# W2 by seven block products in place of eight, in a DeltaNet and MLP kernel

## The chip, the cores and the metric

The kernel runs on one core of one Trainium2 chip. The metric is the device time of one execution in microseconds (us). Before the change, six runs gave a median of 615.64 us, between 613.14 and 621.12.

## The reference

There are two stages. The first is a delta-rule recurrence, for 4 batches and 8 heads of width 48 over 768 tokens; the second is a layer norm and an MLP of width 384 to 1536 to 384 with a residual. All is float32.

```python
for t in range(S):
    kt, vt, bt = (k_n[:, :, t], v[:, :, t], beta[:, :, t, None])
    y[:, :, t] = np.einsum('bhd,bhde->bhe', q[:, :, t], state)
    v_old = np.einsum('bhde,bhd->bhe', state, kt)
    state = state + bt[:, :, :, None] * np.einsum('bhd,bhe->bhde', kt, vt - v_old)
...
x = np.ascontiguousarray(attn_out.transpose(0, 2, 1, 3)).reshape(B, S, H * D)
...
xn = (x - mu) / np.sqrt(var + 1e-06) * g_ln
ch = np.maximum(xn @ w_ch1, 0.0) @ w_ch2
return (x + ch).astype(np.float32)
```

## The kernel before

**Chunks.** The 768 tokens are cut into 12 chunks of 64 (C). A chunk has 256 rows for the MLP (TOK: 4 batches of 64 tokens), in two groups g of 128. Within a chunk the recurrence is made parallel: products of keys with keys and queries with keys (`gram` L368, `product` L393), the inverse of a triangular matrix per head, and a few small matmuls with the carried state s_all.

**The inverse.** From chunk 4 on, two chunks are inverted together in blocks of 32 by a loop on VectorE: 31 steps of one multiply (tmp, L555) and one subtract (xb, L560). Chunks 0 to 3 use blocks of 16, joined to 32 first. At the end `scatter` turns the result (own, L483), fills xt (L468, L472), and `join` (L574 to L631) makes the full block of 64 with two sets of small matmuls on TensorE (p_e L580, p_z L626); x_n (L574) is what p_e multiplies with.

**The recurrence.** `recur` has, for every chunk, p_k and p_y from the state (L652), VectorE's subtraction from v (L657), p_u (L663), the state's update p_s (L675) with VectorE's addition to s_all (L678), the second part of p_y (L683), and then the layer norm's numbers (L694 to L701) and the transposition of its result (p_n, L709; xnt, L710).

**The MLP.** `ffn(c)` first makes h, in 12 blocks of 128 columns: three matmuls into p_h (L724) and ScalarE's Relu into a tile h_f (L730). Then it makes h W2: for each group g, twelve matmuls 128 rows by 384 columns are added up in one PSUM accumulator p_o (L746). VectorE adds the residual x into o (L735), and SyncE stores it in two transfers (L737). Chunk 0 does both groups together, the other chunks one after the other. p_h and p_o take turns in two PSUM buffers (tag "ffn").

**Weights.** W1 and W2 come as 64-bit words and are turned into float32 by ScalarE and VectorE while the first chunks run (`to_fp32`, L313 to L326); the pool "early" holds the raw words and is closed when that is done.

**Order.** The kernel's first part has an order written out by hand. After it, a `Plan` gives every piece of work a due time on a line of its own, where one chunk of the recurrence takes T = 45 steps, and issues the pieces in order of due time. `ffn(c)` is spread in N_FFN = 24 turns (12 for h, 12 for the product) over the T steps that follow the start of chunk c + 1. The inverse of a pair due at t runs from t - 58 to t - 18, its join until t - 2. The framework derives the waits, and on each engine instructions run in the order in which they were queued. VectorE, GpSimd and SyncE are such queues; SyncE carries the loads of q, k and v together with the stores, GpSimd the loads of turned k, the scaling of v (L428) and some clearings.

Of the kernel before, what the change touches and what calls it, by code (L numbers as in the profile page):

```python
# [8 lines left out]
FP32 = mybir.dt.float32  # L9
U32 = mybir.dt.uint32  # L10
U16 = mybir.dt.uint16
ALU = mybir.AluOpType
ACTF = mybir.ActivationFunctionType
# [3 lines left out]
C = 64  # L17
# [76 lines left out]
def kernel(  # L94
# [22 lines left out]
    nc = tc.nc  # L117
# [3 lines left out]
    DM = H * D  # L121
    DFF = w_ch1.shape[1]
    KC = DM // 128
    FT = DFF // 128
    NP = H // 2
    GH = 2 * H
    TOK = 256
# [3 lines left out]
    work = ctx.enter_context(tc.tile_pool(name="work", bufs=2))  # L131
# [15 lines left out]
    def ps_ffn(shape, name):  # L147
        return psum.tile(shape, FP32, name=name, tag="ffn", bufs=2)
# [61 lines left out]
    w2_sb = const.tile([128, FT, DM], FP32, name="w2_sb")  # L210
# [73 lines left out]
    for t in kraws:  # L284
# [5 lines left out]
        out=is_b, in_=ident.rearrange("p (q b s) -> p b q s", b=2, s=FB), axis=mybir.AxisListType.XY, op=ALU.add  # L290
    )
    nc.vector.tensor_reduce(
        out=is_u, in_=ident.rearrange("p (e u s) -> p u e s", u=2, s=BK), axis=mybir.AxisListType.XY, op=ALU.add
# [144 lines left out]
    def prep_v(c):  # L438
        if c > 2:
            load_kv(c)  # L440
        yield
        scale_v(c, norms(c), nc.gpsimd)
        yield
# [267 lines left out]
        yield  # L711


    N_FFN = FT + 2 * FT // 2

    mlp = {}

    def ffn(c):
        xnt, x = xnts.pop(c), xs.pop(c)
        hs = []  # L720
        for f in range(FT):
            p_h = ps_ffn([128, TOK], "p_h")
            for t in range(KC):
                nc.tensor.matmul(  # L724
                    p_h, w1_sb[:, t, f * 128 : (f + 1) * 128], xnt[:, t],
                    start=(t == 0), stop=(t == KC - 1),
                )
            mlp["PE"] = nc.cur_bb.bb.instructions[-1]
            h_f = work.tile([128, TOK], FP32, name="h_f", bufs=FT)
            nc.scalar.activation(h_f, p_h, ACTF.Relu)  # L730
            hs.append(h_f)
            yield
        def store(g, p_o):
            o = work.tile([128, DM], FP32, name="o", bufs=2)
            nc.vector.tensor_tensor(out=o, in0=p_o, in1=x[:, g], op=ALU.add)  # L735
            for e in range(2):
                nc.sync.dma_start(  # L737
                    out=out[2 * e + g, c * C : (c + 1) * C, :], in_=o[e * C : (e + 1) * C]
                )


        for gs in ((0, 1),) if c == 0 else ((0,), (1,)):
            p_os = [ps_ffn([128, DM], "p_o") for g in gs]
            for f in range(FT):
                for g, p_o in zip(gs, p_os):
                    nc.tensor.matmul(  # L746
                        p_o, hs[f][:, g * 128 : (g + 1) * 128], w2_sb[:, f],
                        start=(f == 0), stop=(f == FT - 1),
                    )
                mlp["PE"] = nc.cur_bb.bb.instructions[-1]  # L750
                if f % 2 and f < FT - 1:
                    yield
            for g, p_o in zip(gs, p_os):
                store(g, p_o)
            yield


    NW = len(pieces)
# [88 lines left out]
        load_kv(2)  # L847
        load_beta()

    T = 45  # L850
    starts = [0, 14, 64] + [80 + T * i for i in range(NCH - 2)]
    ends = [2, 26, 80] + starts[4:]
    plan = Plan()
    plan.spread(weights(3, NW // 2), NW // 2 - 3, 0, 10)
    plan.spread(weights(NW // 2, NW), NW - NW // 2, 12, 38)

    plan.once(39, early.close)
    for c in range(NCH):
        t0, t1 = starts[c], ends[c]
        if c > 1:  # L860
            plan.spread(prep_v(c), 2, t0 - 72, t0 - 12)
        if c:
            plan.once(t0, begin, c)
        plan.spread(recur(c) if c else recur_0, N_RECUR if c else 1, t0, t1)
    plan.spread(second(), 7, 0, 14)
    ffn_0 = ffn(0)
    plan.spread(ffn_0, FT, 2, 18, whole=False)
    plan.spread(ffn_0, FT // 2, 20, 42)
    plan.spread(ffn(1), N_FFN, 42, 80)
    for c in range(2, NCH):  # L870
        plan.spread(ffn(c), N_FFN, starts[c + 1], starts[c + 1] + T)
    for m in range(1, NSL):
        chunks = range(SLAB * m, SLAB * m + SLAB)
        t = starts[SLAB * m]
# [55 lines left out]
```

## Time and profile before

| | |
|---|---|
| median of six runs | 615.64 us |
| the profiled execution, its own time | 618.93 us |
| its span, first to last instruction | 617.0 us |
| mean granted TensorE clock | 0.977 |
| TensorE busy, matmuls | 542.7 us |
| of it p_h (L724), 864 matmuls | 208.1 us |
| of it p_o (L746), 576 matmuls | 201.2 us |
| VectorE busy | 322.3 us |
| ScalarE busy | 170.3 us |
| GpSimd busy | 80.0 us |

The profile names the engines PE (TensorE; PEld is its loading of weights), DVE (VectorE), ACT (ScalarE), POOL (GpSimd) and SP (SyncE). The profiled execution is one run, 3.3 us above the median. A row of slices shows 40 equal parts of the span, 15.4 us each, with the busy share in tenths. A group of instructions shows line, engine, operation, output and inputs by the program's names, shapes and count, then busy time and mean length of one in ns, then the idle time of the engine before them and what ended it. A float32 matmul of the code is two matmuls in the profile, and a matmul's recorded length overlaps that of the next, so the step from start to start is what one costs.

### The profile page before, as it was taken

To read this page: it belongs to the slowest core of one execution; us is meant where nothing else is said; L and a number is where in the kernel's file an instruction comes from. 1 tells how busy PE (TensorE), PEld (TensorE's weight loads), DVE (VectorE), ACT (ScalarE), POOL (GpSimd) and SP (SyncE) were. 2 spreads that over 40 slices of the span, in tenths; PEclk is the share of its full clock that TensorE was granted. 3 is DMA by queue.
4 is the path that set the end of the run, shared out by engine and by line. 5 is a ranking of instruction groups with operands and counts; after the bars stand their busy time and mean duration, and the time that the engine had idled before them with its cause. 6 is when DMAs were issued, how large, how long until landed. Compare 5 with 4: busy or idle time off the path is not lost.

```text
span 617.0 us, 20905 instructions
## 1 busy us (share of the span) xinstructions
PE 542.7 (88%) x9512; PEld 405.9 (66%) x9512; DVE 322.3 (52%) x681; ACT 170.3 (28%) x351; POOL 80.0 (13%) x128
## 2 busy tenths in 40 slices
PE   2045886889999959999999999999999999999997
PEld 2035675557767746866857867768758678677673
DVE  5844868992236994229973149953179730201000
ACT  1222352403333205241314332242322142112120
POOL 5000116331040302300302300011000010000000
PEclk9999989988999988999999999999999999999999
DMA  4716979426034610411510510200200000000101
GB/s 53 183 57 150 186 165 242 71 52 97 5 65 78 105 14 18 85 34 27 91 28 16 89 29 15 53 15 16 53 14 15 1 16 15 14 15 1 27 1 26
DMA packets 126919, 34.51 MB, mean 56 GB/s; under 512 B 121184, under 2 KB 124272, under 8 KB 126832
## 3 DMA queue, kind: packets, MB, share of 16 engines
q1 hardware_dynamic: 110256, 19.14, 18.6%
q0 software_dynamic: 3504, 10.25, 6.2%
q10 hardware_dynamic: 13072, 3.80, 2.7%
q8 instruction: 74, 1.21, 0.8%
q14 instruction: 13, 0.11, 0.1%
HBM read 28.44 MB, written 4.72 MB: 54 GB/s over the span
## 4 chain that ended last, share of the span: by engine, by line
PE 57%; DVE 26%; issue 7%; DMA 3%; ACT 3%; SPq 2%; POOL 1%; ACTq 0%; DVEq 0%; POOLq 0%
PE p_h L724 21%; PE p_o L746 19%; DVE tmp L555 8%; DVE xb L560 8%; PE p_g L393 2%; PE p_e L580 2%; PE p_y L683 2%; PE p_g L368 2%; PE p_z L626 2%; DVE kqt L348 2%; PE p_u L663 1%; DVE own L483 1%; SPq L168 1%; PE p_n L709 1%; PE p_s L675 1%
## 5 line engine op out<-in xcount | busy, mean ns | idle before, releaser
L724 PE MATMUL p_h<-xnt,w_sb 128*128 128x256 f32 x864 | 208.1, 395 | 5.5 <-DVE o L735 4.8
L746 PE MATMUL p_o<-w_sb,h_f 128*128 128x384 f32 x576 | 201.2, 498 | 0.0
L724 PEld LDWEIGHTS p_h<-xnt,w_sb 128*128 128x128 f32 x864 | 165.5, 196 | 33.7 <-DVE o L735 4.0
L746 PEld LDWEIGHTS p_o<-w_sb,h_f 128*128 128x128 f32 x576 | 107.5, 193 | 65.5 <-issue 2.7
L730 ACT ACTIVATE h_f<-p_h 128x256 f32<-128x256 f32 x144 | 55.3, 384 | 193.4 <-PE p_h L724 193.4
L168 POOL DMA_DIRECT2D tb<-in_k_dram x64 | 41.9, 662 | 111.1 <-DVE tmp L555 57.3
L560 DVE TENSOR_TENSOR xb<-xb,tmp 128x31 f32<-128x31 f32 (+20 forms) x154 | 51.1, 332 | 5.1
L735 DVE TENSOR_TENSOR o<-p_o,x_ln 128x384 f32<-128x384 f32 x24 | 13.2, 549 | 74.1 <-PE p_o L746 74.1
L555 DVE TENSOR_TENSOR tmp<-xb,gb 128x31 f32<-128x31 f32 (+15 forms) x124 | 42.3, 341 | 3.8
L694 DVE BATCH_NORM_STATS2 st<-x_ln 128x6 f32<-128x384 f32 x24 | 12.3, 546 | 51.5 <-ACT x_ln L688 51.5
L678 DVE TENSOR_TENSOR s_all<-s_all,p_s 128x768 f32<-128x768 f32 x11 | 10.3, 940 | 47.4 <-PE p_s L675 47.2
L348 DVE STREAM_TRANSPOSE kqt<-tb 128x1024 f32<-128x1024 f32 x24 | 29.3, 1231 | 4.1 <-DMA tb<-in_k_dram 3.8
L368 PE MATMUL p_g<-kqt 48*64 48x64 f32 (+2 forms) x1024 | 16.5, 234 | 13.1 <-DVE kqt L348 8.2
L368 PEld LDWEIGHTS p_g<-kqt 48*32 48x32 f32 (+1 forms) x1024 | 14.4, 130 | 18.6 <-DVE kqt L348 8.3
L420 POOL TENSOR_SCALAR knrm<-knrm 128x16 f32<-128x16 f32 x12 | 3.1, 257 | 163.4 <-ACT knrm L419 163.4
L417 DVE TENSOR_REDUCE ksum<-ksq 128x8 f32<-128x384 f32 x22 | 12.1, 550 | 23.3 <-ACT ksq L411 12.9
L610 PE MATMUL p_e<-x_n,gsb 32*32 32x16 f32 x512 | 6.2, 190 | 20.2 <-DVE x_n L605 16.2
L580 PE MATMUL p_e<-x_n,gsb 32*32 32x32 f32 x768 | 16.1, 200 | 7.7 <-DVE mv L695 5.9
L393 PEld LDWEIGHTS p_g<-kqt 48*64 48x64 f32 x768 | 14.7, 148 | 11.8 <-DVE s_all L678 6.5
L580 PEld LDWEIGHTS p_e<-x_n,gsb 32*32 32x32 f32 x768 | 14.7, 113 | 11.1 <-DVE x_n L574 6.0
L393 PE MATMUL p_g<-kqt 48*64 48x64 f32 x768 | 17.2, 237 | 4.9 <-DVE s_all L678 3.9
L657 DVE TENSOR_TENSOR v_raw<-v_raw,p_k 128x768 f32<-128x768 f32 x11 | 10.5, 951 | 20.5 <-PE p_k L652 20.5
(99 smaller groups left out, 510.7 us busy)
## 6 DMA issues: line engine op xcount, KB each, us to landing
words<-in_moe_w_ch_dram POOLq DMA_DIRECT2D x9, 768.0 KB, 5.7
out_dram<-o SPq DMA_DIRECT2D x48, 96.0 KB, 2.2
k<-in_k_dram SPq DMA_DIRECT2D x44, 96.0 KB, 2.7
v_raw<-in_v_dram SPq DMA_DIRECT2D x22, 192.0 KB, 4.0
tb<-in_q_dram SPq DMA_DIRECT2D x44, 64.0 KB, 2.5
words<-in_moe_w_ch_dram ACTq DMA_DIRECT2D x3, 768.0 KB, 5.7
tb<-in_k_dram POOLq DMA_DIRECT2D x32, 64.0 KB, 2.8
tb<-in_q_dram SPq DMA_DIRECT2D x44, 32.0 KB, 2.3
```

The costliest lines, as they stand in the source:

```text
L168: engs[m % len(engs)].dma_start(out=dst[p0 : p0 + 32, :, u, 0:w], in_=src[:, hp::2, toks, 32 * m : 32 * m + w].rearrange("b j t d -> t (b ...
L348: nc.vector.transpose(made[c][0][:, :, n].rearrange("p i (u t) -> p i u t", t=32), tblocks[(2 * c + n) % NTB])
L368: nc.tensor.matmul(out_, kqt[rows, i, 0, r0 : r0 + (BK if fine else C)], kqt[rows, i, 0, r0:C])
L393: nc.tensor.matmul(p_g[half(e ^ hp), hp, j], kqt[rows, i, 0], kqt[rows, i, 1])
L555: nc.vector.tensor_tensor(out=t, in0=xb[:, :, 0:n, j : j + 1].to_broadcast([128, nb, n, w]), in1=gb[:, :, j : j + 1, j + 1 : L].to_broadca ...
L560: nc.vector.tensor_tensor(out=rest, in0=rest, in1=t, op=ALU.subtract)
L580: nc.tensor.matmul(p_e[r1, h], gsb[r0, h, BK:C], xn[r0, h])
L626: nc.tensor.matmul(p_z[r0, h], es[r1, h], xt[r1, h, BK:C])
L724: nc.tensor.matmul(p_h, w1_sb[:, t, f * 128 : (f + 1) * 128], xnt[:, t], start=(t == 0), stop=(t == KC - 1),)
L730: nc.scalar.activation(h_f, p_h, ACTF.Relu)
L735: nc.vector.tensor_tensor(out=o, in0=p_o, in1=x[:, g], op=ALU.add)
L746: nc.tensor.matmul(p_o, hs[f][:, g * 128 : (g + 1) * 128], w2_sb[:, f], start=(f == 0), stop=(f == FT - 1),)
```

## The change

From chunk 1 on, h W2 is made as a product of 2 by 2 blocks with seven block products. With A = h cut by group (rows) and by halves of the 12 blocks (columns), B = W2 cut by the same halves (rows) and by halves of its 384 columns, each block product is six matmuls of 128 rows by 192 columns where the eight of a plain product would be 48 such. Four sums of blocks of W2 (T1 to T4) are made once, by GpSimd, after chunk 0's product; T1 is written over the block W2_12. Four sums of blocks of h (S1 to S4) are made by VectorE in each chunk, three of them over the blocks of h itself. Two PSUM accumulators collect the products: p_a takes products 1, 3, 5 and 7 (1 and 3 add up, and so on), p_cb has in its halves p_c (product 2) and p_b (products 4 and 6). VectorE adds them, as they come, to the residual in the four quarters of the output, each read having to be over before the next product into that accumulator begins. The stores of both groups come after the sixth and seventh products. h is held in two tiles of six blocks. The plan's step T becomes 43, and N_FFN 26.

```diff
-    N_FFN = FT + 2 * FT // 2
+    HF, HM = FT // 2, DM // 2
+    N_FFN = FT + 7 * 2
+    sums = []
+
+    def sum_blocks():
+
+        late = ctx.enter_context(tc.tile_pool(name="late", bufs=1))
+        b11, b12, b21, b22 = (w2_sb[:, i : i + HF, j : j + HM] for i in (0, HF) for j in (0, HM))
+        t2, t3, t4 = (late.tile([128, HF, HM], FP32, name=f"t{i}") for i in (2, 3, 4))
+        for t, x0, x1 in ((t3, b22, b12), (b12, b12, b11), (t2, b22, b12), (t4, b21, t2)):
+            nc.gpsimd.tensor_tensor(out=t, in0=x0, in1=x1, op=ALU.subtract)
+        sums.extend((late, b12, t2, t3, t4))
...
-        hs = []
+        h = [work.tile([128, HF, TOK], FP32, name="h") for _ in range(2)]
...
-            h_f = work.tile([128, TOK], FP32, name="h_f", bufs=FT)
-            nc.scalar.activation(h_f, p_h, ACTF.Relu)
-            hs.append(h_f)
+            nc.scalar.activation(h[f // HF][:, f % HF], p_h, ACTF.Relu)
             yield
...
+        a11, a21, a12, a22 = (h[i][:, :, g * 128 : (g + 1) * 128] for i in range(2) for g in range(2))
+        late, t1, t2, t3, t4 = sums
+        s1, s2, s3, s4 = late.tile([128, HF, 128], FP32, name="s1"), a11, a21, a12
+        add(s1, a21, a22)
+        add(s3, a11, a21, ALU.subtract)
+        p_cb, p_a = ps_ffn([128, DM], "p_o"), ps_ffn([128, HM], "p_a")
+        p_c, p_b = p_cb[:, 0:HM], p_cb[:, HM:]
...
+        def mul(p, a, b, first):
+            for f in range(HF):
+                nc.tensor.matmul(
+                    p, a[:, f], b[:, f], start=(first and f == 0), stop=(f == HF - 1), skip_group_check=True,
+                )
+                mlp["PE"] = nc.cur_bb.bb.instructions[-1]
+                if f == HF // 2 - 1:
+                    yield
+
+
+        yield from mul(p_a, a11, w11, True)
+        add(s2, s1, a11, ALU.subtract)
+        add(o11, p_a, x11)
+        yield
+        yield from mul(p_c, a12, w21, True)
+        add(s4, a12, s2, ALU.subtract)
+        add(o11, p_c, o11)
+        yield
+        yield from mul(p_a, s2, t2, False)
+        add(o12, p_a, x12)
+        yield
+        yield from mul(p_b, s1, t1, False)
+        add(o22, p_b, x22)
+        yield
+        yield from mul(p_a, s3, t3, False)
+        add(o22, p_a, o22)
+        yield
+        yield from mul(p_b, s4, w22, False)
+        add(o12, p_b, o12)
+        store(0)
+        yield
+        yield from mul(p_a, a22, t4, False)
+        add(o21, p_a, x21)
+        store(1)
+        yield
...
-    T = 45
+    T = 43
...
+    plan.once(42, sum_blocks)
```

More of the change, by code (lines that the diff above doesn't have):

```diff
@@ L728, in ffn, with store, add @@
             mlp["PE"] = nc.cur_bb.bb.instructions[-1]
-            h_f = work.tile([128, TOK], FP32, name="h_f", bufs=FT)
-            nc.scalar.activation(h_f, p_h, ACTF.Relu)
-            hs.append(h_f)
+            nc.scalar.activation(h[f // HF][:, f % HF], p_h, ACTF.Relu)
             yield
-        def store(g, p_o):
-            o = work.tile([128, DM], FP32, name="o", bufs=2)
-            nc.vector.tensor_tensor(out=o, in0=p_o, in1=x[:, g], op=ALU.add)
+        os = [work.tile([128, DM], FP32, name="o", bufs=2) for g in range(2)]
+        def store(g):
             for e in range(2):
                 nc.sync.dma_start(
-                    out=out[2 * e + g, c * C : (c + 1) * C, :], in_=o[e * C : (e + 1) * C]
+                    out=out[2 * e + g, c * C : (c + 1) * C, :], in_=os[g][e * C : (e + 1) * C]
                 )
-        for gs in ((0, 1),) if c == 0 else ((0,), (1,)):
-            p_os = [ps_ffn([128, DM], "p_o") for g in gs]
+        def add(out_, in0, in1, op=ALU.add, eng=nc.vector):
+            eng.tensor_tensor(out=out_, in0=in0, in1=in1, op=op)
+        if c == 0:
+            p_os = [ps_ffn([128, DM], "p_o") for g in range(2)]
             for f in range(FT):
-                for g, p_o in zip(gs, p_os):
+                for g in range(2):
                     nc.tensor.matmul(
-                        p_o, hs[f][:, g * 128 : (g + 1) * 128], w2_sb[:, f],
+                        p_os[g], h[f // HF][:, f % HF, g * 128 : (g + 1) * 128], w2_sb[:, f],
                         start=(f == 0), stop=(f == FT - 1),
@@ L752, in ffn @@
                     yield
-            for g, p_o in zip(gs, p_os):
-                store(g, p_o)
+            for g in range(2):
+                add(os[g], p_os[g], x[:, g])
+                store(g)
             yield
+            return
+        a11, a21, a12, a22 = (h[i][:, :, g * 128 : (g + 1) * 128] for i in range(2) for g in range(2))
[5 more added lines that the diff above has]
+        p_c, p_b = p_cb[:, 0:HM], p_cb[:, HM:]
+        x11, x12, x21, x22 = (x[:, g, n : n + HM] for g in range(2) for n in (0, HM))
+        o11, o12, o21, o22 = (os[g][:, n : n + HM] for g in range(2) for n in (0, HM))
+        w11, w21, w22 = w2_sb[:, 0:HF, 0:HM], w2_sb[:, HF:, 0:HM], w2_sb[:, HF:, HM:]
+        def mul(p, a, b, first):
[31 more added lines that the diff above has]
+        yield
     NW = len(pieces)
```

## Prediction

> **What bounds the kernel now.** I read, in this order, the page's busy times, its slices, the groups of instructions, a table of busy time by stretch, and then the order of time around the joins of two chunks.
>
> ```profile
> PE 542.7 (88%) x9512; PEld 405.9 (66%) x9512; DVE 322.3 (52%) x681; ACT 170.3 (28%) x351; POOL 80.0 (13%) x128
> PE   2045886889999959999999999999999999999997
> DVE  5844868992236994229973149953179730201000
> ...
> L724 PE MATMUL p_h<-xnt,w_sb 128*128 128x256 f32 x864 | 208.1, 395 | 5.5 <-DVE o L735 4.8
> L746 PE MATMUL p_o<-w_sb,h_f 128*128 128x384 f32 x576 | 201.2, 498 | 0.0
> ...
> L735 DVE TENSOR_TENSOR o<-p_o,x_ln 128x384 f32<-128x384 f32 x24 | 13.2, 549 | 74.1 <-PE p_o L746 74.1
> L678 DVE TENSOR_TENSOR s_all<-s_all,p_s 128x768 f32<-128x768 f32 x11 | 10.3, 940 | 47.4 <-PE p_s L675 47.2
> ```
>
> From about 160 us on TensorE (PE) is 90% busy or more in nearly every slice, so its work is the bound; the product that is changed (L746) is a third of the span. But VectorE (DVE) comes in waves, with four crests in which it too is full. The next table has a row for each crest and one for the quiet end; its columns are the stretch, its length, then busy time and count of PE, PEld, DVE, ACT and POOL, the granted clock, DMA share and GB/s.
>
> ```profile
> 194.50:230.50 36.00, 29.54 (x507) 22.81 (x505) 33.72 (x84) 5.99 (x14) 6.13 (x9) 0.94 0.42 64
> 277.50:314.30 36.80, 34.61 (x498) 26.37 (x497) 34.64 (x83) 7.05 (x17) 6.11 (x9) 1.00 0.33 56
> 364.00:402.00 38.00, 35.84 (x502) 27.12 (x501) 35.17 (x83) 7.96 (x19) 0.95 (x1) 1.00 0.16 33
> 452.00:488.50 36.50, 34.15 (x497) 26.11 (x496) 33.57 (x81) 6.63 (x17) 0.00 (x0) 1.00 0.05 13
> 546.00:612.60 66.60, 66.52 (x498) 48.81 (x496) 4.94 (x12) 11.97 (x29) 0.00 (x0) 1.00 0.05 13
> ```
>
> The crests are the 32-step inverses (L555, L560), 92 to 94% busy, the rest being the hand-over from one short instruction to the next. How near they are to ending last, the order of time shows (start, length, engine, line, and in brackets the idle time before it and its releaser):
>
> ```profile
> 230.55 1.92 PE L580 MATMUL p_e<-x_n,gsb 32*32 32x32 f32 x64 [5.86 <-DVE mv L695]
> ...
> 311.63 1.16 PE L393 MATMUL p_g<-kqt 48*64 48x64 f32 x64 [1.26 <-DVE s_all L678]
> ...
> 313.04 1.29 DVE L574 STREAM_TRANSPOSE x_n<-xt 128x512 f32<-128x512 f32 x2
> ...
> 320.09 0.59 PE L580 MATMUL p_e<-x_n,gsb 32*32 32x32 f32 x25
> ```
>
> In the first crest PE already waits 5.86 us for VectorE. In the second the last thing that VectorE makes for the join, x_n, is done at 314.3 and PE comes for it at 320.1: 5.8 us of room.
>
> **What is taken away.** In the quiet end matmuls run back to back, which gives their step. 48 of 128x384 take 15.64 us with the last one's 0.49 hanging over: 15.15/47 = 322 ns. 72 of 128x256: (15.70 - 0.38)/71 = 216 ns. Six transposes of 128x128, each with its own weights: (0.82 - 0.27)/5 = 109 ns. That is a line, 0.83 ns a column and 2 ns, so 128x192, halfway between the last two, should step at 162 ns. A matmul in the code is two in the profile (576 for 288). A chunk's product now costs 48 x 322 = 15.48 us; seven blocks of six are 84 x 162 = 13.64. Gain 1.84 us a chunk, 20.2 us over eleven.
>
> **Weights.** 48 loads become 84. Their rows say 190 to 196 ns each, longer than 162. If a load held its matmul up for all of that, a chunk would cost 84 x 0.196 = 16.5 us, 1.0 more than now, 11 us in all. I take 162, because the transposes' loads last 141 ns in the profile and still step at 109: the recorded length isn't what a load occupies. [...]
>
> **The start of a chunk's products.** The two accumulators p_cb and p_a take the two buffers of the last two p_h. If p_a, which goes first, gets the newer one, PE waits for its Relu: about 0.75 us (384 ns and two hand-overs, as 596.9 to 597.5 in the quiet end); nothing if it gets the older one or the recurrence's matmuls stand between. 0 to 8 us over eleven; I take 2.
>
> **VectorE.** Four sums of 128x768 at 0.95 (L678) are 3.8 us, eight adds of 128x192 at about 0.35 (between L735's 0.55 and the 0.36 of a 128x192 step of the inverse) 2.8 us; two adds of 0.55 go. That is 5.5 us more a chunk, 60 us in all, 322 to 383. PE now waits for VectorE before the third to seventh product and the next p_h; what covers each wait is one product, 1.95 us. A quiet VectorE answers in 0.15 + 0.35 us, or 0.15 + 0.95 + 0.35 where a sum goes first, so outside the crests this costs nothing: chunks 1, 9, 10, 11 wholly, 3, 5, 7 mostly. Chunks 2, 4, 6, 8 meet a crest, where everything stands in one queue. Some 4.9 us of the 5.5 fall before x_n there.
> First crest: PE waits for its end now, so it ends 4.9 us later, less if some of the sums slide behind it: 1 to 7, I take 5, with the chunk's own gain mostly lost in it.
> The other three: 5.8 us of room less 4.9 less the 1.84 that PE comes earlier is a wait of about 1 at p_e, and waits inside (the s_all of 311.6 had stood 5.7 us in the queue). 0 to 5 each; I take 1.5, 4.5 for the three.
>
> **GpSimd's four sums, once.** 128x1152 each; its one such row is L428, 1,477 ns for 128x768, so 2.2 us each and 8.9 us. They wait for w2 (done at 119) and, from the second on, for chunk 0's last product (about 132); the second operand is needed by chunk 1's third product near 170, so GpSimd itself is in time. Behind them in its queue may stand the scaling of v for chunk 2 (done at 131.8, first used at 171.9), and then a clearing of es at 147.4, after the last sum by 138.6. Not free is what they do to VectorE:
>
> ```profile
> 130.18 0.28 DVE L555 TENSOR_TENSOR tmp<-xb 128x120 f32<-128x120 f32 x1
> 130.50 1.46 DVE L560 TENSOR_TENSOR xb<-xb,tmp 128x120 f32<-128x120 f32 x1
> 131.99 0.27 DVE L555 TENSOR_TENSOR tmp<-xb 128x110 f32<-128x110 f32 x1
> ...
> 130.34 1.48 POOL L428 TENSOR_TENSOR v_raw<-v_raw,knrm 128x768 f32<-128x768 f32 x1
> ```
>
> While GpSimd's one ran, a VectorE step of 0.28 took 1.46. Four sums could hold the 16-step inverse, which ends at 141 with PE coming for it at 142.3, for up to 8.9 us, or miss its two-operand steps altogether. 0 to 8; I take 3. [...]
>
> **At nothing.** The step 45 to 43 and 26 turns for 24 change only the order; PE's time per chunk falls from 43.5 to 41.7, in step with it. Both stores now follow the last products, so SP's loads that stood behind the first store pass it, and those behind both come up to 6 us later; VectorE waited 3.8 us in the whole run for such a load (L348), which is the price if the cover is gone.
>
> **The sum.** 20.2 - 2 - 5 - 4.5 - 3 = 5.7 us less. The profiled run took 618.9 (span 617.0 and 1.9 around it), 3.3 above the median; on the median: 615.6 - 5.7 = 609.9. With every term at its good end 19 less, 596; with all at the bad end 20.2 - 8 - 7 - 15 - 8, that is 18 more, 633. Likely within the case: 604 to 616.
>
> **Rivals.**
> VectorE has room after all (22%): crest sums slide into the pauses around 263 to 277 and 320 on, GpSimd's sums fall beside transposes and PSUM reads. For it: VectorE is 52% busy, and 383 of 600 us is still no bound. Against: queue order, and the 5.86 us wait. Left: 20.2 less 3 to 8, 598 to 603.
> The queue of VectorE becomes the bound in the crests (23%): each of the four ends 4.9 us later, none of the room is usable because PE is held inside the products that stand before p_e, and each chunk's 1.84 is lost there: 4 x 6.7 = 27, with 2 for the buffers and 6 for GpSimd: 15 slower, 630. It decides once all waits pass 20 us together; below 26 it still reads as no change. For it: s_all's 5.7 us in the queue. Against: three crests had 5.8 us of room.
> Weight loads show (5%): 196 ns a step, 31 us worse than my sum, 640.
> The change removes less than it says (5%): PE idles elsewhere for what it saves, 615. The count of matmuls speaks against it: 9,512 must become 9,512 + 11 x 36 = 9,908 with L746's columns down an eighth.
>
> **Numbers.** My case 45%, 20 of these below 609.5. About 1%, 6 us, is what a measurement tells from no change. Faster 20 + 22 = 42%; same 25 + 5 + 5 (the mild end of the queue) = 35%; slower 18 + 5 = 23%. Range 599 to 626: it leaves out the best of the first rival, and the worse half of the second with the weight loads.
>
> **What would show it.** Matmuls 128x192 stepping at 162 (or 190) ns in the quiet end; that end (chunks 9 to 11) shorter by 5.5 us; PE's wait before the first p_e near 230 growing from 5.9 to about 11; waits of PE for the S sums in the crests; steps of L560 over 1 us near 120 to 140; in the quiet end a gap of 0.75 us before each chunk's first product. I am wrong if the crests' waits don't grow, or if chunks 9 to 11 don't gain.

## The result and the profile after

The changed kernel is slower: 620.01 us, the median of 33 runs, against 615.58 for 73 runs of the kernel before. The ratio is 1.0075, with a 95% interval of 1.0055 to 1.0096, so 3.4 to 5.9 us were lost where 5.7 had been forecast as won. Ratios here leave out runs over 1.5% above the fastest of their kernel, medians take in all of them (one of the 33 took 2,860 us). The profiled execution took 619.03 us.

The page's busy times, its slices and its groups of instructions, for the changed kernel, and below them one group of the kernel before:

```profile
PE 530.1 (86%) x9908; PEld 463.1 (75%) x9908; DVE 381.9 (62%) x780; ACT 170.2 (28%) x351; POOL 90.2 (15%) x132
PE   2046997848899978999969999899999799999997
DVE  5846878996175997249993279984179951321312
...
L735 PE MATMUL p_h<-xnt,w_sb 128*128 128x256 f32 x864 | 205.6, 392 | 9.7 <-DVE o L752 9.1
L787 PE MATMUL p_a<-t,h 128*128 128x192 f32 x396 | 72.5, 329 | 0.2 <-DVE v_raw L657 0.2
L787 PE MATMUL p_o<-w_sb,h 128*128 128x192 f32 x264 | 52.7, 346 | 0.0
L678 DVE TENSOR_TENSOR s_all<-s_all,p_s 128x768 f32<-128x768 f32 x11 | 10.3, 938 | 52.6 <-PE p_s L675 52.6
L393 PE MATMUL p_g<-kqt 48*64 48x64 f32 x768 | 19.6, 258 | 16.7 <-DVE s_all L678 11.7
L787 PE MATMUL p_o<-w_sb,s 128*128 128x192 f32 x132 | 25.6, 339 | 4.7 <-DVE o L752 4.7
```

```profile
L393 PE MATMUL p_g<-kqt 48*64 48x64 f32 x768 | 17.2, 237 | 4.9 <-DVE s_all L678 3.9
```

The count is the 9,908 that the prediction asked for, and TensorE's busy time has gone down by 12.6 us (the mean granted clock was 0.957 against 0.977, and matmuls at half clock are busy for longer: p_g's 314 ns each from 400.5 to 407.5 us, where the clock was 0.51, against 221 from 313 to 320, where it was 1.00). The span hasn't: TensorE now waits 11.7 us before p_g (L393) for s_all and 4.7 us before the fourth product for the additions into o; before the change, the wait of p_g for s_all was 3.9 us. VectorE's busy time grew by 59.6 us, where 60 had been worked out; that the two agree is luck, since part of it is time in which VectorE was held up: with GpSimd's sums held back (below) it is 373.4, so the work itself grew by 51.1.

To see where the time went, I took from the order of time the start of each chunk's first p_h in both profiles. A stretch runs from one chunk's start of h to the next one's, so it holds that chunk's own product. After minus before, in us:

| until chunk 0's h | chunks 0 and 1 | chunks 2, 4, 6, 8 (with a 32-step inverse, a crest) | chunks 3, 5, 7, 9, 10 | chunk 11 to the end | span |
|---|---|---|---|---|---|
| -2.4 | +5.2 | -0.3, +2.2, +3.1, +3.2: +8.2 | -9.0 | -1.9 | 0.0 |

The first column isn't the change's: it varies from -7.2 to +0.5 over all the kernels below. The spans of the two profiled executions agree (617.0), but that of before lay 3.3 us above its median and that of after 1.0 below.

**The light chunks** gained what was worked out. The order of time at the end (start, length, engine, line, operation, tiles, count):

```profile
595.77 3.19 PE L735 MATMUL p_h<-xnt,w_sb 128*128 128x256 f32 x14
598.79 2.11 PE L787 MATMUL p_a<-w_sb,h 128*128 128x192 f32 x12
```

Twelve matmuls take 2.11 us with the last one's 0.33 hanging over: 1.78/11 = 162 ns. The first product follows p_h with no gap. Each light stretch is 1.70 to 1.83 us shorter.

**Chunks 0 and 1** hold GpSimd's four sums. The order of time there, VectorE's long steps and GpSimd's sums together, then TensorE's two long waits (in brackets the idle time before, and who ended it):

```profile
115.91 2.69 POOL L724 TENSOR_TENSOR t<-w_sb 128x1152 f32<-128x1152 f32 x1 [7.53 <-DVE nrm L541]
117.27 1.38 DVE L544 TENSOR_TENSOR db<-nrm 128x32 f32<-128x32 f32 x1
120.60 2.61 POOL L724 TENSOR_TENSOR w_sb<-w_sb 128x1152 f32<-128x1152 f32 x1 [1.40 <-PE p_o L759]
120.70 2.61 DVE L555 TENSOR_TENSOR tmp<-xb 128x78 f32<-128x78 f32 x1
123.34 3.24 DVE L560 TENSOR_TENSOR xb<-xb,tmp 128x78 f32<-128x78 f32 x1
123.81 2.67 POOL L724 TENSOR_TENSOR t<-w_sb 128x1152 f32<-128x1152 f32 x1
126.62 3.25 DVE L555 TENSOR_TENSOR tmp<-xb 128x96 f32<-128x96 f32 x1
127.10 2.65 POOL L724 TENSOR_TENSOR t<-w_sb,t 128x1152 f32<-128x1152 f32 x1
...
133.61 0.33 PE L393 MATMUL p_g<-kqt 48*64 48x64 f32 x4 [4.13 <-DVE pt L395]
139.80 2.47 PE L735 MATMUL p_h<-xnt,w_sb 128*128 128x256 f32 x5 [5.87 <-DVE o L752]
```

Beside every sum stands one VectorE instruction that ends 0.05 to 0.12 us after it: 120.70 + 2.61 = 123.31 against 120.60 + 2.61 = 123.21, and so on. Those steps take 0.24 to 0.26 us, and L544 0.19, when nothing stands beside them. Lost: 1.2 + 2.4 + 3.0 + 3.0 = 9.6 us of VectorE, at a place where TensorE waits for what follows.

**The crests.** The order of time of the one near 310, first three lines of before (with 311.63, 313.04 and 320.09 in the prediction), then those after the change:

```profile
277.43 1.95 DVE L477 STREAM_TRANSPOSE gb<-gsb 128x1024 f32<-128x1024 f32 x1 [2.54 <-ACT gsb L383]
308.68 2.09 DVE L483 STREAM_TRANSPOSE own<-xb 128x1024 f32<-128x1024 f32 x1
310.67 0.91 DVE L678 TENSOR_TENSOR s_all<-s_all,p_s 128x768 f32<-128x768 f32 x1
```

```profile
278.98 1.94 DVE L477 STREAM_TRANSPOSE gb<-gsb 128x1024 f32<-128x1024 f32 x1
...
310.42 2.01 DVE L483 STREAM_TRANSPOSE own<-xb 128x1024 f32<-128x1024 f32 x1
312.33 0.90 DVE L678 TENSOR_TENSOR s_all<-s_all,p_s 128x768 f32<-128x768 f32 x1
313.28 1.16 PE L393 MATMUL p_g<-kqt 48*64 48x64 f32 x64 [3.02 <-DVE s_all L678]
...
319.31 0.68 DVE L574 STREAM_TRANSPOSE x_n<-xt 128x512 f32<-128x512 f32 x1
...
321.61 1.24 PE L787 MATMUL p_o<-w_sb,s 128*128 128x192 f32 x6 [1.69 <-DVE o L752]
...
323.88 1.20 PE L580 MATMUL p_e<-x_n,gsb 32*32 32x32 f32 x64
```

s_all stands in VectorE's queue behind the last steps of the inverse and the transposition of its result. The inverse itself, from its first step (gb) to the end of own, isn't longer: 33.4 us, and 33.3 before. It is TensorE that gets through its own work beside it sooner. Before the change TensorE waited 1.26 us for s_all; now it comes 1.76 us earlier against VectorE and waits 3.02 (1.25 became 2.95 in chunk 6, 1.44 became 3.25 in chunk 8). So the gain of 1.84 has become a wait almost whole. Only in chunk 2 is the inverse longer, 38.3 us against 34.9. The fourth product waits another 1.69 for an addition that stood behind pt, x_n and a sum of blocks of h. And x_n is done at 320.0 where p_e comes at 323.9: the room that the prediction counted on is still there, 3.9 us of it, and nobody uses it.

After two of these waits the clock falls. The table by stretch (stretch, length, busy time and count of PE, PEld, DVE, ACT, POOL, granted clock, DMA share, GB/s):

```profile
400.50:407.50 7.00, 6.66 (x136) 6.01 (x137) 6.88 (x12) 0.50 (x1) 0.51 (x1) 0.51 0.01 4
489.00:496.00 7.00, 6.41 (x135) 5.76 (x136) 5.22 (x7) 0.25 (x1) 0.00 (x0) 0.53 0.01 2
313.00:320.00 7.00, 6.64 (x152) 5.87 (x152) 7.00 (x13) 0.80 (x1) 0.44 (x1) 1.00 0.01 2
```

Behind the waits of 2.95 and 3.25 us (chunks 6 and 8) TensorE had half its clock for 6.8 us, behind the one of 3.02 (chunk 4) it kept all of it. The kernel before had waits of 1.25 to 1.44 us there and no half clock in these chunks.

### The profile page after: what moved, and what is told of

Same layout as the page of the kernel before. It is cut to its first block, busy times and chain, and to the rows that moved or that the text cites. A ratio compares the mean times of both kernels' runs of the same rounds, so it can differ in the third digit from the quotient of the medians.

```text
span 617.0 us, 21798 instructions
## 1 busy us (share of the span) xinstructions
PE 530.1 (86%) x9908; PEld 463.1 (75%) x9908; DVE 381.9 (62%) x780; ACT 170.2 (28%) x351; POOL 90.2 (15%) x132
## 3 DMA queue, kind: packets, MB, share of 16 engines
q8 instruction: 77, 1.26, 0.8%
## 4 chain that ended last, share of the span: by engine, by line
PE 36%; DVE 19%; ACT 3%; issue 2%; DVEq 0%; ACTq 0%
PE p_h L735 16%; PE p_a L787 7%; PE p_o L787 6%; DVE tmp L555 5%; DVE xb L560 5%; PE p_y L683 2%; PE p_g L393 1%; DVE own L483 1%; DVE o L752 1%; ACT ksq L413 1%; DVE gb L477 1%; DVE h L752 1%; PE p_u L663 1%; PE p_k L652 1%; PE p_y L652 1%
## 5 line engine op out<-in xcount | busy, mean ns | idle before, releaser
L735 PE MATMUL p_h<-xnt,w_sb 128*128 128x256 f32 x864 | 205.6, 392 | 9.7 <-DVE o L752 9.1
L735 PEld LDWEIGHTS p_h<-xnt,w_sb 128*128 128x128 f32 x864 | 163.5, 194 | 35.1 <-issue 6.0
L740 ACT ACTIVATE h<-p_h 128x256 f32<-128x256 f32 x144 | 55.2, 383 | 188.3 <-PE p_h L735 180.6
L787 PE MATMUL p_a<-t,h 128*128 128x192 f32 x396 | 72.5, 329 | 0.2 <-DVE v_raw L657 0.2
L787 PEld LDWEIGHTS p_a<-t,h 128*128 128x128 f32 x396 | 64.2, 190 | 0.9 <-issue 0.3
L787 PE MATMUL p_o<-w_sb,h 128*128 128x192 f32 x264 | 52.7, 346 | 0.0
L787 PEld LDWEIGHTS p_o<-w_sb,h 128*128 128x128 f32 x264 | 45.7, 200 | 1.0
L678 DVE TENSOR_TENSOR s_all<-s_all,p_s 128x768 f32<-128x768 f32 x11 | 10.3, 938 | 52.6 <-PE p_s L675 52.6
L393 PE MATMUL p_g<-kqt 48*64 48x64 f32 x768 | 19.6, 258 | 16.7 <-DVE s_all L678 11.7
L393 PEld LDWEIGHTS p_g<-kqt 48*64 48x64 f32 x768 | 16.9, 166 | 21.8 <-DVE s_all L678 12.9
L787 PE MATMUL p_o<-w_sb,s 128*128 128x192 f32 x132 | 25.6, 339 | 4.7 <-DVE o L752 4.7
L787 PEld LDWEIGHTS p_o<-w_sb,s 128*128 128x128 f32 x132 | 21.9, 194 | 5.5 <-DVE o L752 5.3
L752 DVE TENSOR_TENSOR s<-h 128x768 f32<-128x768 f32 x11 | 10.5, 952 | 24.6 <-ACT h L740 24.6
```

The costliest lines, as they stand in the source:

```text
L393: nc.tensor.matmul(p_g[half(e ^ hp), hp, j], kqt[rows, i, 0], kqt[rows, i, 1])
L735: nc.tensor.matmul(p_h, w1_sb[:, t, f * 128 : (f + 1) * 128], xnt[:, t], start=(t == 0), stop=(t == KC - 1),)
L740: nc.scalar.activation(h[f // HF][:, f % HF], p_h, ACTF.Relu)
L752: eng.tensor_tensor(out=out_, in0=in0, in1=in1, op=op)
L787: nc.tensor.matmul(p, a[:, f], b[:, f], start=(first and f == 0), stop=(f == HF - 1), skip_group_check=True,)
```

## The experiments

Theory: GpSimd's sums hold VectorE in the inverse of chunks 2 and 3, and in the crests VectorE, not TensorE, sets the pace, so that TensorE's saving turns into waits. Rivals: the work of VectorE's four sums of blocks of h is the price; or the order of issue (the step T) is; or the waits can simply be taken out by moving s_all. All times are medians, and the ratios are to runs of the kernel before on the same chip.

A table of the stretches of all profiles, against the kernel before as above, stands first, since the runs are read with it.

| kernel | chunks 0 and 1 | 2, 4, 6, 8 | 3, 5, 7, 9, 10 | ratio and interval |
|---|---|---|---|---|
| the change | +5.2 | +8.2 | -9.0 | 1.0075 (1.0055 to 1.0096) |
| sums due later | +5.1 | +8.0 | -9.0 | 1.0094 (1.0058 to 1.0130) |
| sums on VectorE | -1.3 | +8.0 | -9.0 | 0.9918 (0.9867 to 0.9968) |
| sums held back | -5.4 | +10.9 | -9.0 | 0.9917 (0.9878 to 0.9957) |
| before, with the sums added | +13.3 | -0.3 | 0.0 | 1.0145 (1.0084 to 1.0205) |
| sums held, none of h | -4.0 | +8.4 | -9.1 | 0.9965 (0.9928 to 1.0002) |
| sums held, s_all first | -2.7 | +9.2 | -9.0 | 0.9886 (0.9830 to 0.9943) |
| the same, copies on ScalarE | -4.7 | +7.4 | -9.0 | 0.9879 (0.9832 to 0.9926) |
| sums on VectorE, copies on ScalarE | -2.0 | +6.3 | -9.0 | 0.9873 (0.9817 to 0.9930) |
| before, s_all first, copies on ScalarE | +1.4 | -4.4 | 0.0 | 0.9913 (0.9875 to 0.9952) |
| the change with T = 45 | +7.3 | +17.7 | -9.0 | 1.0225 (1.0183 to 1.0267) |
| before with T = 43 | -0.2 | +7.2 | 0.0 | 1.0165 (1.0114 to 1.0216) |
| sums held, T = 41 | -5.8 | +3.2 | -6.2 | 0.9911 (0.9874 to 0.9948) |
| plain products in crests | +3.8 | +3.0 | -9.0 | 0.9987 (0.9952 to 1.0021) |
| sums held, plain in crests | -4.9 | +4.1 | -9.0 | 0.9764 (0.9704 to 0.9823) |
| the same, copies on ScalarE | -5.8 | +6.3 | -9.0 | 0.9776 (0.9709 to 0.9843) |
| sums held, plain in crests, s_all first | -2.8 | -1.7 | -9.0 | 0.9764 (0.9683 to 0.9846) |
| the same, copies on ScalarE | -6.2 | -4.5 | -9.0 | 0.9761 (0.9699 to 0.9822) |

The stretches are of one profiled execution each. The eight kernels with the sums held and all of h's sums differ little up to chunk 1, and yet that column runs from -2.7 to -6.2 for them, so a single profile tells it to some 3.5 us.

### GpSimd's sums

Due later in the plan:

```diff
-    plan.once(42, sum_blocks)
+    plan.once(57, sum_blocks)
```

> GpSimd's four sums are made at step 57 of the plan in place of 42, behind the inverse of chunks 2 and 3. Theory (VectorE is held up): the sums block VectorE's two-operand steps, which shows as steps of 2.6 to 3.3 us between 117 and 130 and as gaps of 4.1 and 5.9 us on TensorE; moved, the time falls by about 9 us, to 611 (ratio to the kernel before about 0.993), and no step of the 16-step inverse takes over 1.5 us. Rival (the order of the plan, step 43 with 26 turns, costs the time): 620, ratio 1.0075, as with the change.

620.71 us. The edit failed: nothing ahead of them in GpSimd's queue held the sums back, so they still ran from 114 to 127 us, VectorE's steps beside them took 1.4 to 3.5 us, and TensorE's two waits were 6.36 and 5.72. A due time in the plan orders what is queued; it doesn't hold an instruction back. It tells nothing of either theory.

On VectorE:

```diff
-            nc.gpsimd.tensor_tensor(out=t, in0=x0, in1=x1, op=ALU.subtract)
+            nc.vector.tensor_tensor(out=t, in0=x0, in1=x1, op=ALU.subtract)
```

> The same four sums at the same place, by VectorE itself. Theory: 4 x 1.36 us (128x1152 at VectorE's rate for 128x768, 0.95 us) stand in its queue in place of some 9 us of being blocked, so 620 - 9 + 5 = 616. Rival (it is the waiting of the sums for chunk 0's product, wherever they are made, that costs): no better than 620, more if VectorE's queue stands still behind a sum.

613.41 us. The four take 1.30 to 1.36 us each on VectorE itself, 5.4 in all, and no step of the inverse is longer than 1.2 us; the wait of 5.87 before p_h shrinks to 0.86. The time is below the 616 of the theory, and far from the rival's 620. The crests stay at +8.0.

On GpSimd, with an edge in the issue order that puts them behind the scaling of v for chunk 3:

```diff
     def scale_v(c, knrm, eng):
...
+        scaled[c] = nc.cur_bb.bb.instructions[-1]
...
+    def behind_scale(fn):
+        with behind(tc, {0: scaled[3]}):
+            fn()
...
-    plan.once(42, sum_blocks)
+    plan.once(57, behind_scale, sum_blocks)
```

> GpSimd's four sums are put behind its scaling of v for chunk 3 by an edge of order (their due time alone left them at 114 to 127 us, where they were). They should run from about 157 to 168, after both 16-step inverses. Theory (the sums block VectorE): no step of the inverse over 1.5 us but the one beside the scaling of v, TensorE's gaps of 6.4 and 5.7 us before the first h of chunk 1 down to about 2, and the time 9 us less than with the change, 611, at or below the kernel with VectorE's sums (613.4). Rival (the gain of VectorE's sums came from a changed order, not from the lifted block): 616 or more.

609.46 us. The order of time on GpSimd:

```profile
145.39 1.47 POOL L430 TENSOR_TENSOR v_raw<-v_raw,knrm 128x768 f32<-128x768 f32 x1
146.82 2.68 POOL L732 TENSOR_TENSOR t<-w_sb 128x1152 f32<-128x1152 f32 x1
149.58 2.62 POOL L732 TENSOR_TENSOR w_sb<-w_sb 128x1152 f32<-128x1152 f32 x1
152.28 2.69 POOL L732 TENSOR_TENSOR t<-w_sb 128x1152 f32<-128x1152 f32 x1
155.04 2.73 POOL L732 TENSOR_TENSOR t<-w_sb,t 128x1152 f32<-128x1152 f32 x1
```

The same four sums, as long as before, now run while TensorE does the joins and VectorE has a pause of 7.5 us (one later step, L471, is held beside them: 1.86 us for its usual 0.49). Chunks 0 and 1 are 10.6 us shorter than in the changed kernel (-5.4 against +5.2), of which chunk 2 gives 2.7 back (+2.3 after -0.3). The ratio falls by 0.0158, that is 9.7 us, or 7 to 12 with both intervals.

And the sums alone, in the kernel before, into tiles that nothing reads:

```diff
+        for t, x0, x1 in ((t3, b22, b12), (t1, b12, b11), (t2, b22, t1), (t4, b21, t2)):
+            nc.gpsimd.tensor_tensor(out=t, in0=x0, in1=x1, op=ALU.subtract)
...
+    plan.once(42, sum_blocks)
```

> The kernel before, with GpSimd's four sums added at the place where the change has them, into tiles that nothing reads: no seven products. Theory (the sums alone hold VectorE's two-operand steps of the 16-step inverses): 8 to 10 us slower, 623 to 626 (1.013 to 1.016), with steps of L555 and L560 of about 3 us beside the sums. Rival (the price comes only together with the seven products): within 2 us of the kernel before.

626.44 us, 1.0145: 8.9 us slower (5.2 to 12.6); the profiled run, of 632.8, was the longest of the six, which is why the table has +13.3. The time is as the theory has it, but the instructions that were held are others than expected. The order of time:

```profile
122.94 1.40 DVE L544 TENSOR_TENSOR db<-nrm 128x32 f32<-128x32 f32 x1
124.37 2.62 DVE L545 TENSOR_TENSOR db<-db,beta_f 128x32 f32<-128x32 f32 x1
127.02 3.74 DVE L546 TENSOR_TENSOR xb<-xb,db 128x512 f32<-128x512 f32 x1
130.69 2.83 DVE L549 COPY xb<-db 128x32 f32<-128x32 f32 x1
133.56 0.19 DVE L555 TENSOR_TENSOR tmp<-xb 128x30 f32<-128x30 f32 x1
```

Here the sums met the inverse's preparation, where the four take 0.19, 0.19, 0.69 and 0.28 in the kernel before: 9.2 us more. One instruction is held for each sum, the copy with its single input too. So GpSimd's sums cost some 9 us without a single one of the seven products.

### The sums of h

The products take the plain blocks of h in place of S1 to S4, which aren't made, so the output isn't a product with W2 any more:

```diff
-        s1, s2, s3, s4 = late.tile([128, HF, 128], FP32, name="s1"), a11, a21, a12
-        add(s1, a21, a22)
-        add(s3, a11, a21, ALU.subtract)
+        s1, s2, s3, s4 = a22, a11, a21, a12
...
-        add(s2, s1, a11, ALU.subtract)
...
-        add(s4, a12, s2, ALU.subtract)
```

> As the kernel whose sums are held, but without VectorE's four sums of h in each chunk (44 instructions of 0.95 us): the products take the blocks as they are. Theory (VectorE's queue in the inverses is the loss over chunks 2, 4, 6, 8): the start of h moves 1.8 us earlier per chunk in these chunks too, no gap of 3 us on TensorE before p_g, and the time is 615.6 less 20 and 2 to 3 more, 594 to 598. Rival (the eight adds from PSUM, each awaited by the next product, are the loss): no better than 606.

610.33 us, against 609.46 with the sums of h. Taking 42 us of work from VectorE (11 x 4 x 0.95) gained nothing that the intervals show, where the theory had 594 to 598: the waits before p_g were 4.35 us in chunks 4 and 6 (3.01 and 3.02 with the sums). In these chunks the inverse takes 33.4 us with the sums of h and without; TensorE comes earlier and waits for the same inverse. So work on VectorE isn't the price by itself. Nor is it the additions from PSUM, the rival: no product in chunks 4, 6 and 8 waits over 0.2 us for one here. Only in chunk 2 do the sums lie within the inverse (38.3 us with them, 35.1 without), and that stretch is 2.9 us shorter without them.

### The place of s_all, and the copies

s_all goes ahead of the last steps of the 32-step inverse (on the kernel with held sums):

```diff
+            with behind(tc, {0: updates[c]} if j == 28 else {}):
...
             nc.vector.tensor_tensor(out=s_all, in0=s_all, in1=p_s, op=ALU.add)
+            updates[c] = nc.cur_bb.bb.instructions[-1]
```

> As the kernel whose GpSimd sums are held (609.5), with VectorE's addition to s_all put before the last three steps of the 32-step inverse in its queue, by an edge of order. Theory now: over the inverses TensorE is paced by VectorE's chain, its gain of 1.8 us turns into a longer wait of p_g for s_all (3.0 us against 1.3), and the wait of 3 us brings half clock. With s_all earlier that wait falls from 3.0 to 0.5 or less in three inverses, half clock near 393 and 482 goes, and the time is 4 to 10 us less, 600 to 606. Rival (VectorE's chain paces TensorE whatever stands in it, so the wait only moves on to the join's p_e): 608 to 611, with a new wait of 2 us at p_e or a product.

608.25 us. The waits of its TensorE from 120 us on (who, for what, us in all, times, longest):

```profile
PE p_o L799 <- DVE o L764: 10.3, 4, 3.0
PE p_h L747 <- DVE o L764: 5.0, 5, 1.9
PE p_g L393 <- DVE s_all L684: 2.5, 1, 2.5
PE p_e L616 <- DVE x_n L611: 1.1, 1, 1.1
PE p_a L799 <- DVE h L764: 2.0, 2, 1.0
```

The waits for s_all fall from 11.8 us to 2.5, which is the first crest's, and those of the fourth product rise from 4.7 to 10.3. The wait moved on into the product, as the rival had it, in chunks 4 and 6 (+3.8 each, after +2.2 and +3.1); chunk 8 gained 4.0, and the crests are at +9.2 after +10.9. The same with the copies of L472 on ScalarE, and the copies so moved with the sums on VectorE:

```diff
-                to_xt(SLAB * m + i, nc.vector)
+                to_xt(SLAB * m + i)
```

> The same and the copies of the inverted blocks on ScalarE, 0.8 us less of VectorE per inverse. Theory: another 0 to 4 us, 598 to 605. Rival: no more than 1 us.

607.20 us: waits of some 0.97 and of 2.56 us are left within the products of each of chunks 4 and 6, one of 1.95 in chunk 8.

> VectorE makes the sums of W2, and the two copies of the inverted blocks per chunk pair in the 32-step inverses (0.41 us each) go to ScalarE. Theory: VectorE's queue before s_all and the sums of h gets 0.8 us shorter in each of four inverses, and with that TensorE's wait of 3.0 us and the half clock after it; 613.4 less 3 to 8, 605 to 610. Rival (the wait is for the transposition own and the adds ahead of it, which stay): 612 to 614.

605.43 us, 0.9873 (0.9817 to 0.9930). That is in the theory's range, but not by the theory's way: chunks 4 and 6 wait for s_all as long as before, 3.02 and 2.97 us, and only chunk 8 is shorter (+0.2 after +3.1). From the 0.9918 without the copies it isn't clear of the intervals.

The kernel before with both, and without seven products:

> The kernel before, with s_all put first and the copies on ScalarE, and nothing of the change. If these two mend a wait that the change made, it gains at most the 1.3 us of each inverse: 611 to 616. If they mend the kernel before as much: 604 to 608, and the change itself is worth only the difference.

609.83 us, 0.9913. There the same edge and copies gain 4.4 us in the crests, and no wait for s_all is left. So what the changed kernel wins by mending (0.9879) is hardly more than what the kernel before wins by it: with seven products everywhere, the products' own worth was within the intervals.

### The step T

```diff
-    T = 43
+    T = 45
```

> The change with the plan's step at 45 as before. Theory: 620 within 2 us, the step only sets an order. Rival (order): the time comes back to 612 or below.

628.91 us: the wait at s_all is 1.42 again, but the products wait 2.48 and 1.20 in chunk 4, 2.48 and 2.76 in chunk 6. The crests cost +17.7.

> The kernel before with the plan's step at 43 alone. With 45 the changed kernel took 629, so the order weighs. Theory (the step must follow TensorE's time per chunk): at 43, too short for 43.5 us a chunk, the kernel before gets slower, 618 or more. Rival (a shorter step gives the inverses a larger share of the time and helps any kernel): faster, 612 or less.

623.34 us: the kernel before with T = 43 loses 7.2 us in the crests, with waits of 3.3 us for s_all in chunks 4 and 6, though it has no product of the new kind. Behind the first of them (3.32) TensorE had half its clock for 6.8 us (the 64 matmuls of p_g took 1.99 us, against 1.16 at 311.63 before), behind the second (3.33) the whole of it: the two stretches are 5.6 and 2.9 us longer.

> As the kernel whose GpSimd sums are held, with the plan's step at 41. The step was worth 9 us from 45 to 43 with the change and cost 8 from 45 to 43 without. If the order is what decides and 43 is at its best place: 613 or more. If a shorter step still spreads the inverses better: under 606.

609.25 us, as with 43 (609.46): in the profile, the fastest run of its twelve, the crests gain 7.8, and three light stretches lose half of their gain. The step, which the prediction put at nothing, decides where TensorE waits in a crest: it is worth 9 us in the changed kernel (45 against 43), 10 the other way in the kernel before, and nothing from 43 to 41.

### Plain products in the crests

Chunks 2, 4, 6 and 8 by eight products, in the changed kernel, where W2_12 holds T1, so that these chunks' right halves are made with T1 in its place:

```diff
+    PLAIN = (0, 2, 4, 6, 8)
...
-        if c == 0:
+        if c in PLAIN:
```

> Chunks 2, 4, 6 and 8, whose products fall into the 32-step inverses, are multiplied plainly as before; chunks 1, 3, 5, 7, 9, 10, 11 with seven products; the sums stay where they are. Theory: the start of h of chunks 4 to 9 came later than before by 2.2, 3.1 and 3.2 us over chunks 4, 6 and 8; plain they cost nothing more than before, so 620 - 8 = 612. Rival (order): 620. Second rival (the light chunks pay it back later): over 616.

615.86 us. The crests fall from +8.2 to +3.0, though four products are dearer by 1.84 each; chunks 0 and 1 still have the sums beside the inverse (a wait of 7.60 there). With the sums held, and the right halves put right by W2_12 = T1 + W2_11, which needs only the left half of the first six blocks to be added on:

```diff
+                    if i == 0:
+                        add(x[:, g, HM:], p_os[g][:, 0:HM], x[:, g, HM:])
+                    else:
+                        add(os[g], p_os[g], x[:, g])
+                        store(g)
```

> GpSimd's sums held as in the run that put them behind the scaling of chunk 3, and chunks 2, 4, 6 and 8 by eight plain products again, with the sum W12 + W22 - W11 put right by adding the left half's A11 W11 part into the right half of x. Theory (VectorE's chain paces TensorE in the crests, so plain products lose nothing there and spare the waits of about 3 us and the half clock behind them): the waits before p_g fall to about 1.4 us, and the time is 603 to 607 (0.98 to 0.987). Rival (the seven products are worth as much in the crests as elsewhere, and the waits would be there anyhow): 4 times 1.8 us slower than the run with the sums held, 614 to 617 (1.00).

603.39 us, 0.9764 (0.9704 to 0.9823): below the run with seven products everywhere (0.9878 to 0.9957) with no overlap. The rival had 614 to 617. Chunks 4 and 6 wait 1.43 us for s_all. Chunk 8 waits 2.58, then has half the clock for 3.4 us behind it, and costs +3.25 where 4 and 6 cost +0.65.

> The same with the copies of the inverted blocks on ScalarE. Theory (VectorE paces the crests, and the copies are some 2 us of each crest's chain): another 1 to 4 us less than with the copies on VectorE, 600 to 605. Rival (TensorE has become the bound in the crests with plain products): no change.

604.62 us, 0.9776: no gain from the copies alone, as the rival had it (in the profile chunk 8 is at +5.9, with a wait of 3.51 in its product).

> Plain products in chunks 2, 4, 6 and 8 and the sums held, and besides the addition to s_all put ahead of the last steps of the 32-step inverse. Theory (with plain products TensorE asks nothing of VectorE within the product, so the wait before p_g, 1.43 in chunks 4 and 6 and 2.58 in chunk 8, isn't moved on but gone, as in the kernel before with the same edge): the crests of chunks 4, 6 and 8 shorter by 1.3 to 1.4, 1.3 to 1.4 and about 4 us, no half clock near 475, 595 to 600 (0.965 to 0.972). Rival (the wait moves on to x_n or to o, as it did with seven products): within 2 us of the run without the edge.

597.89 us, 0.9764. The waits for s_all in chunks 4, 6 and 8 are gone and haven't come back as others (0.45 and 0.47 us for pt are all that is left before p_g), and after 232 us the clock stays whole until the last microseconds (the 64 matmuls of p_g at 310.46 take 1.16 us). Chunk 8 is 4.3 us shorter, as the theory had it; chunks 4 and 6 only 0.8 instead of 1.3. The ratio is no better than that of the kernel without the edge, with an interval of 1.6% (its runs of before spread from 607 to 619); between the two profiles, from chunk 0 on, it is 3.7 us.

> The same with the copies of the inverted blocks on ScalarE. Theory of a bound by VectorE's chain: again 1 to 3 us less. Rival (nothing of the chain is waited for any more): no change.

597.01 us, 0.9761 (0.9699 to 0.9822), the same as without the copies (597.89). Its busy times, and the two longest of its TensorE's waits from 120 us on:

```profile
PE 528.7 (89%) x9764; PEld 435.2 (73%) x9764; DVE 355.8 (60%) x744; ACT 174.8 (29%) x359; POOL 90.6 (15%) x132
```

```profile
PE p_h L748 <- DVE o L765: 4.1, 5, 0.9
PE p_g L393 <- DVE s_all L684: 1.5, 1, 1.5
```

It is the fastest kernel found, some 2.4% below the kernel before and 3.1% below the changed one (0.9761/1.0075 = 0.969). TensorE does only 1.4 us less than in the changed kernel, on four chunks the dearer product; it waits less. The light chunks' -9.0 now stays. Against the kernel before with the same edge and copies (0.9913) the seven products are worth 1.5% here, some 9 us (5 to 14 with both intervals); in that comparison they sit in seven chunks and would give 12.9 at 1.84 each.

## Why the prediction was wrong, point by point

**The gain, 20.2 us: right.** 162 ns a step, 1.70 to 1.84 us a light chunk. The load rows of 190 to 200 ns weren't what a load occupies, so that rival is out. The end, chunks 9 to 11, is 5.5 us shorter, as forecast, and the count was right. VectorE's busy time of 383 was met by luck: the work grew by 51, 4.6 a chunk and not 5.5, and the rest is time held up.

**The start of a chunk's products, 2 us: nothing.** p_a got the older buffer: its first matmul starts at 598.79, just behind p_h's last, and the Relu that reads the last p_h only at 598.99.

**GpSimd's sums, 3 us: this term failed.** It was 9 to 10 (9.7 by holding them back, 8.9 with the sums alone, each with an interval of some 3 us either way; the two profiles alone show 7.0, the +5.2 of chunks 0 and 1 with chunk 1's gain of 1.84), at or beyond the 8 that the prediction allowed. It took 2.2 us for a sum, which took 2.61 to 2.73, and let some of them miss VectorE's two-operand steps. But each sum held the first such step that came during it, or just ahead of it, until it was over, and with short steps queued one after the other there always was one: the hold was nearly the whole length of all sums (9.6 of 10.6 us). In two of four cases the step was held even from 0.47 us before the sum, while GpSimd was issuing a load (0.65 us, from 123.15 and 126.44). The row of before that the term was made from, a step of 1.46 beside a GpSimd instruction of 1.48, had already shown the hold to be whole.

Which of the two started first didn't decide who waited: the steps begun at 117.27 and 120.70 came after the sums of 115.91 and 120.60, those begun at 123.34 and 126.62 before the sums of 123.81 and 127.10, and all four ended 0.05 to 0.12 us after the sum.

A sum of blocks of h never met a scaling of v, and the longest of the 44 such sums took 0.96 us.

**The first crest, 5 us: too dear.** Chunk 2 got 0.31 shorter, where its gain alone makes 1.84: a price of 1.5. Its inverse did end later, by 3.4 us of the 4.9. The 5.86 at p_e, which was to grow to 11, went away, and 2.52 at p_g and 3.03 at the fourth product took its place; what is waited for earlier needn't be waited for at p_e again.

**The other three crests, 1.5 us each: the second step that failed.** They cost 4.1, 4.9 and 5.1 (+2.22, +3.06 and +3.22 with 1.84 added), the upper end of its bounds. "5.8 us of room less 4.9 less the 1.84 ... is a wait of about 1 at p_e" looked at the wrong wait. The room at x_n was there after the change too, but TensorE is stopped ahead of it, at s_all and inside the product. That s_all was late already (1.26) stood in the lines of the prediction; each microsecond that TensorE comes earlier there is a microsecond waited. The second rival had this half right: the room is of no use because TensorE is held in front of it, and each chunk's 1.84 is lost. But it had each crest end 4.9 us later, and the three later inverses are as long as before (33.4 us against 33.3 in chunk 4): the sums of h stand behind the inverse, not in it. So its sum (27 us for four crests) was too high, the measured price being 15.5.

**At nothing, the step 45 to 43: not nothing.** The kernel before loses some 10 us by it (1.0165), the changed one would be 9 us slower without it (1.0225 against 1.0075). What a step does depends on the rest, and this couldn't be read off the count of work.

**The sum as measured.** 20.2 - 0 - 1.5 - 14.0 - 9.7 is 5.0 us slower; 4.4 were measured. The bound of 1% for "the same" holds it, the interval shows it as a loss.

How much of a crest's price is the half clock? In chunk 4 none: the changed kernel kept its full clock there and paid 4.1. The runs with the sums due later and on VectorE had 3.4 us at half clock behind the same wait, and the stretch took them 49.13 and 49.17 us, against 49.16; the fourth product's wait was 0.3 us in place of 1.69, so what the half clock took was waited for anyway. Chunk 6, with 6.8 us of it, cost 0.8 more than chunk 4. What stays open is chunk 8: in the run with plain products the half clock there is at most 2.6 us (+3.25 against +0.65), of which 1.15 is the longer wait itself.

## What to carry to other kernels

A saving on the busiest engine is worth what it is only in stretches where that engine ends last; where it already waits for another, even 1.3 us, the saving was added to the wait here (1.26 us became 3.02), so look for the first such wait in each stretch and not for the room at the last. A cheap algorithm with more hand-overs belongs where the other engines are quiet: here in seven of eleven chunks, with eight plain products in the four others and the sums in a pause, it won 2.4% (s_all first and the copies added nothing that the intervals show). Work put on GpSimd beside a chain of short VectorE steps cost VectorE nearly its full length here (9.6 of 10.6 us), so put it into one of VectorE's pauses, by an edge in the issue order and not by a due time.

## What the hardware showed unexpectedly

Half a clock after short waits: those of 2.95 and 3.25 us in the changed kernel were followed by 6.8 us at half clock each, its 2.52 and 3.03 in chunk 2 by 3.4 us each (from 223.2 and from 233.4 us), and 2.58 by 3.4 us in the run with plain products and held sums (a clock of 0.57 from 475 to 479), while 3.02 us in chunk 4 was followed by none. So the length of the wait alone doesn't decide: 2.52 had half a clock behind it and 3.02 hadn't. What decides, and why the stretches are 3.4 and 6.8 us long, these runs don't show.

A copy of 128x32 on VectorE, one input and 0.19 us long by itself (L549, six in the changed kernel, 188 ns on average), took 2.83 us beside a GpSimd sum in the kernel before with the sums added, like the steps with two inputs. A transposition of 1.24 us beside the first sum of the changed kernel took its usual 1.24, and an addition of 128x192 with one input in PSUM its usual 0.35 beside the scaling of v at 244.47.
